# Delta-rule attention and a gelu feed-forward on one core: the first two chunks rebuilt

## The chip, the core and the metric

The kernel runs on one core of a Trainium2 chip. The metric is the device time of one execution in microseconds; the median of three runs is 825.52 us (823.81 to 825.66). The engines of the core work side by side: TensorE (PE in the profile, with PEld for its weight loads), VectorE (DVE), ScalarE (ACT), GpSimd (POOL) and SyncE (SP), which here only starts transfers.

## The reference

The first half is a delta rule for 4 batches and 8 heads, 768 positions and 48 channels a head. Every head has a state of 48 x 48; keys are normalized. The second half takes all heads of a position as a row of 384 and sends it through two weight matrices with a gelu between them.

```python
for t in range(S):
    kt, vt, bt = (k_n[:, :, t], v[:, :, t], beta[:, :, t, None])
    y[:, :, t] = np.einsum('bhd,bhde->bhe', q[:, :, t], state)
    v_old = np.einsum('bhde,bhd->bhe', state, kt)
    state = state + bt[:, :, :, None] * np.einsum('bhd,bhe->bhde', kt, vt - v_old)
...
x = attn_out.transpose(0, 2, 1, 3).reshape(B * S, H * D)      # 3072 x 384
h = x @ w_in                                                  # 384 x 2048
g = h * (1.0 / (1.0 + np.exp(-1.702 * h)))
return g @ w_out                                              # 2048 x 384
```

The two weight matrices arrive as 64-bit floats and have to be turned into 32-bit floats on the chip.

## The kernel before

**Units.** Positions are cut into 6 chunks of 128. A *unit* is one chunk of one batch, with all 8 heads; unit n is chunk n // 4 of batch n % 4, so there are 24. The units of one batch depend on each other through the state `ST`, those of one chunk do not. Two neighbouring units (`HB` = 2) are a *pair*, and the feed-forward takes a pair at a time.

**What a unit needs.** Keys (`KN`) are normalized (`normalize`, or `normalize_first` for the first seven), turned on TensorE and copied to `kT` (`transposed`). `prepare` (L350 on) multiplies `kT` with itself to the 128 x 128 scores `G` of each head, writes all of `G` to DRAM (`Nd`, 512 KB a unit) and reads back from it only the four 32 x 32 blocks on the diagonal of every head, into `NT`. There a row of 128 lanes holds a block: 4 batches x 8 heads x 4 blocks. `invert` (L389 on) solves these small triangular systems on DVE by substitution, in 25 parts that a caller can draw one after another: one product with beta, 15 rows, 4 and 4 products of quarters, and the last, which multiplies with beta again (`YS`) and takes the result through DRAM (`Yd`) into `XB`. For chunk 0 it runs once for all 128 lanes, for every later chunk twice, with the 64 lanes of a pair.

A `Step` then does the unit itself. `scores` turns the queries and makes `psQ` (the masked scores `M`, and for chunk 1 on the part of V that the state explains). The four blocks of 32 rows follow one another: `solve` multiplies V with `XB` on TensorE (`psU`), ScalarE copies the result to `US`, `below` makes what the block adds to later rows (`psR`), and DVE subtracts that from V (`rest`). `together` puts a `solve` of one unit beside a `below` of another. Last come `queries`, `outputs` and `state` (`psY`, `psS`). `outputs` puts the unit's row block into `xT`; a quarter of its rows goes there by transfers of 16 rows (`xT<-last`).

**Feed-forward.** `hidden` (x @ w_in and gelu, 16 portions a pair) and `written` (times w_out and out, 16 portions a pair) wait in `queue`, and `take` draws portions from it, so TensorE has them between the steps of the units.

**Order.** The kernel is written out as slots. Up to n = 5 `slot` has six groups (`GR`), each with some attention, some steps of `invert`, some conversions (`weights`, after the table `WB`) and some feed-forward; from n = 6 (`W`) `woven` has three stretches, spends 20.8 us of feed-forward a slot, and lets unit n + 1 begin, unit n go on and unit n - 1 end in the same slot. `follow` asks for later inputs, and puts a finished pair into the queue. In slots 0 and 1 and from 6 on the instructions keep the written order on their engines (`pinned`, seen as L105 in the profile); in between the compiler's planner orders them.

**Weights.** `from_double` makes a 32-bit float of the two words of a 64-bit one with four or five DVE instructions and one on ScalarE. A part is 512 columns of one third of w_in, or one of 16 row blocks of w_out. The raw words lie where w_out will be; `free` and `taken` say when a place may be filled again, and GpSimd's queue fetches.

**Before the first slot** (`warm(NW)` on) the keys of four units are normalized in two groups, their scores made and sent through DRAM, three parts of w_in converted, three units scored, and chunk 0's substitution run; matmuls without a result (`ps_warm`) keep TensorE running meanwhile.

Of the kernel before, what the change touches and what calls it, by code (L numbers as in the profile page):

```python
# [18 lines left out]
def kernel(  # L19
# [33 lines left out]
    GR = 6  # L53
    NTH = HB * C
    FQ = 4
    GB = 4

    W0, W1, WB = 3, 1, (1, 3, 5, 7, 8)
    NA = W0

    NW, NA0, NY, NB0 = 80, 3, 48, 6
    XR = DP - D
    W = 6
    NS = C * C + C
    assert S % C == 0 and H == 8 and D <= DP and DM == H * D == KC * 128
    assert B == 4 and B * H * NB == 128 and FC == 4 * FQ
# [40 lines left out]
    in_order, now = [False], [0]  # L107

    class Engine:
# [5 lines left out]
        def __getattr__(self, name):  # L115
            op = getattr(self.engine, name)
            return pinned(op) if in_order[0] else op

    vec, act, pe = Engine(nc.vector), Engine(nc.scalar), Engine(nc.tensor)

    for i in range(B):
        nc.vector.memset(KN[i][:, :, D:DP], 0.0)
        load(i, ((KN, k),))

    bI = cpool.tile([128, NC, BS], F32, name="bI")
    betas = beta.rearrange("b h (c k j) -> (b h) c k j", k=NB, j=BS)
    for blk in range(NB):
        nc.scalar.dma_start(out=bI[blk::NB], in_=betas[:, :, blk, :])


    ident = cpool.tile([128, 128], F32, name="ident")
    make_identity(nc, ident)
    half = cpool.tile([128, H], F32, name="half")
    nc.gpsimd.memset(half, 0.5)

    nc.gpsimd.memset(YB, 0.0)
    nc.gpsimd.affine_select(
        out=YB, in_=YB, compare_op=ALU.not_equal, fill=1.0, base=0,
        pattern=[[1, BS], [-1, BS]], channel_multiplier=0,
    )  # L140


# [5 lines left out]
    def warm(n, after=None):  # L148

        ps = ps_moe.tile([128, 256], F32, tag="moe", name="ps_warm")  # L150
        if after is not None:
            after(ps[:, 0:1], 0.0)
        for _ in range(n):
            pe.matmul(ps, lhsT=ones[:, 0:128], rhs=ones, start=True, stop=True)  # L154

    warm(NW)
    table = cpool.tile([128, 1], F32, name="table")
    nc.scalar.activation(table, ident[:, 0:1], ACT.Copy)

    w_in = cpool.tile([128, KC, DFF], F32, name="w_in")  # L160
# [3 lines left out]
    nc.gpsimd.memset(low, -896.0 * (1 << 23))  # L164

    def from_double(dst, raw, n, alone):

        lo, hi = raw[:, :, 0], raw[:, :, 1]
        ts, stt = vec.tensor_scalar, vec.scalar_tensor_tensor
        if alone:
            ts, stt = pinned(ts), pinned(stt)
        AND, OR = ALU.bitwise_and, ALU.bitwise_or
        E1 = 1 << 20
        p = dst.bitcast(I32)  # L180

        ts(p, hi, 0x7FF * E1, None, op0=AND)
        if alone:
            ts(p, p, -896.0 * E1, 0.0, op0=ALU.add, op1=ALU.max)
            ts(p, p, 255.0 * E1, 8.0, op0=ALU.min, op1=ALU.mult)
        else:
            act.activation(p, p, ACT.Relu, scale=8.0, bias=low)
        yield
        t = wk.tile([128, n], I32, tag="P", name="tmp")
        f = t.bitcast(F32)  # L190
        ts(t, hi, E1 - 1, E1, op0=AND, op1=OR)
        stt(out=f, in0=lo.bitcast(U32), scalar=2.0**-32, in1=t, op0=ALU.mult, op1=ALU.add)
        stt(out=p, in0=hi, scalar=-(1 << 31), in1=p, op0=AND, op1=OR)
        stt(out=dst, in0=f, scalar=2.0**-20, in1=dst, op0=ALU.mult, op1=ALU.mult)
        yield

    N_IN = 512
    parts_in = KC * DFF // N_IN
    n_parts = parts_in + FC

    x_rows = [
        (ct * DP + o, (ct * NP + i) * D, m, step)
        for ct in range(2)
        for o, i, m, step in ((0, 0, D, D), (D, KC, XR, XR))
    ]

    stages, taken, made, begun = {}, {}, [], {}  # L210

    def stage(part):

        if part < parts_in:
            at = part % (2 * KC) * 2 * N_IN
            return at, at + 2 * N_IN
        f = part - parts_in
        if f >= FC - 2:
            return None
        depth = 2 if f < 2 or f >= 8 else 4  # L220
        if f >= 12:
            depth = 1
        at = FC * DM // (2 if f < 2 else 1) - (f % depth + 1) * 2 * DM
        return at, at + 2 * DM

    def together_with(part):

        return list(range(part, part + (KC if part < 3 * KC else 1)))

    def free(part):  # L230
        places = [s for p in together_with(part) if (s := stage(p)) is not None]
        return all(s[1] <= a or b <= s[0] for s in places for a, b in taken.values())

    def fetch(part, dma):

        if part < parts_in:
            j, f0 = part % KC, part // KC * N_IN
            parts = together_with(part)
            shape, src = (len(parts), N_IN), moe_w_in[:, f0 : f0 + N_IN]
            dst = w_in[:, j : j + len(parts), f0 : f0 + N_IN]  # L240
        else:
            parts = [part]
            shape, src = (1, DM), moe_w_out
            dst = target(part)
        if src.dtype != F32:
            if (s := stage(part)) is None:
                raw = wk.tile([128, *shape, 2], I32, tag="xT", name="raw", bufs=3)
            else:
                words = slice(s[0], stage(parts[-1])[1])
                raw = w_out.rearrange("p f d -> p (f d)")[:, words].bitcast(I32)  # L250
                raw = raw.rearrange("p (j n o) -> p j n o", j=shape[0], o=2)
            for i, p in enumerate(parts):
                stages[p] = raw[:, i]
                if s is not None:
                    taken[p] = stage(p)
            dst = raw.bitcast(src.dtype).rearrange("p j n o -> p j (n o)")
        if part < parts_in:
            for i in range(len(parts)):
                for p, r, m, step in x_rows:
                    dma(out=dst[p : p + m, i], in_=src[r + (j + i) * step : r + (j + i) * step + m])  # L260
        else:
            r = (part - parts_in) * 128
            dma(out=dst if src.dtype == F32 else dst[:, 0], in_=src[r : r + 128, :])
        return parts

    def target(part):
        if part < parts_in:
            j, f0 = part % KC, part // KC * N_IN
            return w_in[:, j, f0 : f0 + N_IN]
        return w_out[:, part - parts_in, :]  # L270

    def begin(part):

        if part not in begun:
            if part >= parts_in:
                a, b = (part - parts_in) * DM, (part - parts_in + 1) * DM
                if any(taken[p][0] < b and a < taken[p][1] for p in stages if p in taken):
                    return
            dst = target(part)
            begun[part] = from_double(dst, stages[part], dst.shape[-1], part < NA)  # L280
            next(begun[part])

    def convert(part):
        if part in stages:
            begin(part)
            if staged:
                begin(min(staged))
            stages.pop(part)
            next(begun.pop(part))

            made.append(part)
            while made and (len(made) > 1 or part < NA or part >= n_parts - 8):
                taken.pop(made.pop(0), None)

# [20 lines left out]
    def normalize_first(b0, nb=HB):  # L315

        tt, ts = pinned(vec.tensor_tensor), pinned(vec.tensor_scalar)
        red, recip = pinned(vec.tensor_reduce), pinned(vec.reciprocal)
        stt = pinned(vec.scalar_tensor_tensor)
        mult, add = ALU.mult, ALU.add  # L320
        z = wk.tile([128, 4, nb, H], F32, tag="ksq", name="z", bufs=1)
        x, y, t, s = (z[:, i] for i in range(4))
        for b in range(nb):
            K = KN[(b0 + b) % len(KN)][:, :, 0:D]
            sq = wk.tile([128, H, D], F32, tag="G", name="sq", bufs=6)
            tt(sq, K, K, op=mult)
            red(s[:, b], sq, axis=AX.X, op=add)
# [8 lines left out]
        recip(s, s)  # L336
        for b in range(nb):
            K = KN[(b0 + b) % len(KN)][:, :, 0:D]
            tt(K, K, s[:, b].broadcast_to([128, H, D]), op=mult)

    def transposed(src, dst, early=False):

        pool_, tag = (ps_seq, "seq") if early else (ps_big, "big")
        psT = pool_.tile([128, NP, 128], F32, tag=tag, name="psT")
# [5 lines left out]
    def prepare(n):  # L350

        c, b = units[n]
        kn = KN[n % len(KN)]
        kT = wk.tile([128, NP, 128], F32, tag="kT", name="kT", bufs=6)
        transposed(kn, kT, c == 0)
        yield 0.6
        G = wk.tile([128, H, 128], F32, tag="G", name="G", bufs=6)
        pool_, tag = (ps_moe, "moe") if c == 0 and b % 2 else (ps_big, "big")
# [8 lines left out]
        if n < 2 * B + HB:  # L367
            act.activation(G[:, 1::2], ps[1], ACT.Copy)
        else:
            vec.tensor_copy(G[:, 1::2], ps[1])  # L370

# [357 lines left out]

    def slot(n, share):  # L730

# [197 lines left out]
```

## Time and profile before

| | |
|---|---|
| median of the timed runs | 825.52 us |
| the profiled execution, whole | 821.86 us |
| its span in the profile | 819.8 us |
| first scores on DVE / first `psU` on TensorE | 31.0 / 67.4 us |
| first `ph` of the feed-forward | 103.3 us |
| last `po` | 795.6 to 816.4 us |
| DVE, first 240 us, busy | 57.3 + 25.9 + 119.5 us |
| `w_out<-in_moe_w_out_dram`, 384 KB, issue to landing | 3.7 us median |
| `pow` on GpSimd | 2.2 us mean |

A matmul of 32-bit floats is two records in the profile: 96 records `ph` are the 48 matmuls of one pair. Rows of the timeline give start, duration, engine, line, operation, result and inputs with their shape, how many, and in square brackets how long the engine had been idle and what ended that. L105 is the line of the helper that pins an instruction, so names of tiles tell more than lines.

### The profile page before, as it was taken

What the parts mean: (1) busy time and instruction counts of PE and PEld (TensorE: products, weight loads), DVE (VectorE), ACT (ScalarE), POOL (GpSimd) and SP (SyncE); (2) the same over time, 40 slices, a digit from 0 to 9 for tenths busy, and PEclk for the clock granted to TensorE, in tenths of its full rate; (3) what the DMA queues carried; (4) which work ended last, traced back from release to release, by engine and by line L of the source; (5) the groups of instructions that cost most, each with busy time, mean ns of one, the idle gap of its engine ahead of it and who ended that gap; (6) DMA issues with size and microseconds to landing.
All of it is one profiled execution on the core that took longest, in us unless ns stands there. A gap on an engine that the chain in (4) does not pass through costs nothing.

```text
span 819.8 us, 18780 instructions
## 1 busy us (share of the span) xinstructions
PE 768.8 (94%) x8100; PEld 577.4 (70%) x8100; DVE 483.0 (59%) x1037; ACT 230.7 (28%) x499; POOL 131.7 (16%) x138
## 2 busy tenths in 40 slices
PE   8429799889799999999999999999999999999998
PEld 7327688557676876867867867867768768677684
DVE  7797989787965675666667667666656730100000
ACT  2212543242232332322422322322322223212120
POOL 2013120322021222122123122212201000000000
PEclk9659889978979999999999999999999999999999
DMA  7986732721315123214204213213222020000000
GB/s 146 199 183 122 201 87 82 178 68 48 68 30 125 34 49 96 60 23 100 62 21 102 53 32 90 54 43 80 53 59 45 12 51 1 11 16 1 24 1 19
DMA packets 147698, 55.96 MB, mean 68 GB/s; under 512 B 114720, under 2 KB 143616, under 8 KB 147616
## 3 DMA queue, kind: packets, MB, share of 16 engines
q1 hardware_dynamic: 139872, 41.96, 24.0%
q0 software_dynamic: 2752, 10.62, 4.7%
q10 hardware_dynamic: 4992, 2.20, 1.0%
q8 instruction: 63, 1.03, 0.6%
q14 instruction: 19, 0.16, 0.1%
HBM read 33.13 MB, written 20.45 MB: 65 GB/s over the span
## 4 chain that ended last, share of the span: by engine, by line
PE 79%; DVE 6%; issue 6%; DMA 4%; SPq 2%; POOL 1%; ACT 1%; DVEq 0%; POOLq 0%; ACTq 0%
PE po L105 28%; PE ph L105 25%; PE psY L105 5%; PE psU L105 4%; PE psQ L105 3%; PE ps_warm L154 3%; PE ph L633 2%; PE psG L105 2%; PE psR L105 2%; DMA w_out<-in_moe_w_out_dram 2%; PE psT L105 1%; SPq L105 1%; DMA w_out<-in_moe_w_in_dram 1%; DVE tmp L105 1%; PE psG L362 1%
## 5 line engine op out<-in xcount | busy, mean ns | idle before, releaser
L105 PE MATMUL po<-w_out,gT 128*128 128x384 f32 x704 | 239.3, 490 | 0.0
L105 PE MATMUL ph<-xT,w_in 128*128 128x256 f32 x966 | 222.0, 384 | 0.3
L105 PEld LDWEIGHTS ph<-xT,w_in 128*128 128x128 f32 x966 | 180.3, 191 | 30.9 <-issue 2.3
L105 PEld LDWEIGHTS po<-w_out,gT 128*128 128x128 f32 x704 | 130.1, 190 | 82.6 <-issue 1.9
L105 DVE TENSOR_TENSOR V<-V,psR 64x384 f32<-64x384 f32 (+1 forms) x80 | 44.4, 556 | 194.8 <-PE psR L105 194.0
L105 DVE TENSOR_TENSOR P<-NT,YB 64x18 f32<-64x18 f32 (+25 forms) x171 | 82.3, 481 | 4.5
L105 ACT ACTIVATE gT<-ph 128x512 f32<-128x512 f32 x81 | 48.2, 595 | 115.9 <-PE ph L105 115.8
L105 DVE TENSOR_REDUCE YB<-P 64x6 f32<-64x18 f32 (+25 forms) x171 | 72.7, 425 | 5.5
L105 ACT COPY US<-psU 32x384 f32<-32x384 f32 x80 | 37.6, 470 | 131.9 <-PE psR L105 118.4
L528 POOL TENSOR_SCALAR_AFFINE_SELECT M<-M 128x1024 f32<-128x1024 f32 x24 | 29.8, 1240 | 226.6 <-DVE M L105 159.8
L105 PEld LDWEIGHTS psU<-V,XB 32*32 32x32 f32 x1280 | 45.9, 105 | 27.9 <-issue 20.5
L105 PE MATMUL psU<-V,XB 32*32 32x48 f32 x1280 | 54.3, 203 | 2.1 <-DVE V L105 2.1
L105 PE MATMUL psR<-US,G 32*32 32x48 f32 x1920 | 52.8, 203 | 0.0
L633 PE MATMUL ph<-xT,w_in 128*128 128x128 f32 (+1 forms) x282 | 47.0, 321 | 1.6 <-DMA xT<-last 1.6
L105 PEld LDWEIGHTS psR<-US,G 32*32 32x32 f32 x1920 | 44.6, 105 | 0.5 <-issue 0.5
L633 PEld LDWEIGHTS ph<-xT,w_in 128*128 128x128 f32 x282 | 40.3, 198 | 5.7 <-issue 2.4
L154 PE MATMUL ps_warm<-ident 128*128 128x256 bf16 x152 | 22.8, 318 | 16.7 <-DVE ps_warm L105 14.4
L90 POOL DMA_DIRECT2D KN<-in_k_dram x14 | 13.4, 955 | 153.1 <-PE psY L105 102.0
L308 POOL TENSOR_TENSOR rn<-ssq,half 128x8 f32<-128x8 f32 x17 | 36.9, 2169 | 2.9 <-DVE ssq L306 2.9
L105 ACT COPY o<-po 128x384 f32<-128x384 f32 x22 | 10.5, 479 | 77.7 <-PE po L105 55.8
L154 PEld LDWEIGHTS <-ident 128*128 128x128 bf16 x152 | 17.1, 114 | 21.0 <-issue 14.6
L105 DVE TENSOR_TENSOR P<-NT 64x256 f32<-64x256 f32 (+7 forms) x36 | 30.3, 841 | 0.3
(144 smaller groups left out, 871.0 us busy)
## 6 DMA issues: line engine op xcount, KB each, us to landing
Nd<-G SPq DMA_DIRECT2D x20, 512.0 KB, 3.5
w_out<-in_moe_w_out_dram POOLq DMA_DIRECT2D x14, 384.0 KB, 3.7
QP<-in_q_dram SPq DMA_DIRECT2D x24, 192.0 KB, 3.9
V<-in_v_dram SPq DMA_DIRECT2D x24, 192.0 KB, 3.0
out_dram<-o SPq DMA_DIRECT2D x24, 192.0 KB, 1.9
w_out<-in_moe_w_in_dram SPq DMA_DIRECT2D x18, 192.0 KB, 5.2
NT<-Nd SPq DMA_DIRECT2D x24, 128.0 KB, 2.6
Yd<-YS SPq DMA_DIRECT2D x24, 128.0 KB, 2.5
```

Of the source, the lines that this page charges most:

```text
L90: dma(out=dst[n % len(dst)][:, :, 0:D], in_=src[b, :, c * C : (c + 1) * C, :].rearrange("h p d -> p h d"),)
L105: return lambda *a, **kw: tc.keep_in_program_order(op(*a, **kw))
L154: pe.matmul(ps, lhsT=ones[:, 0:128], rhs=ones, start=True, stop=True)
L308: nc.gpsimd.tensor_tensor(rn, ssq, half, op=ALU.pow)
L362: pe.matmul(ps[h % 2][:, h // 2], lhsT=kT[r, h // 2, :], rhs=kT[r, h // 2, :], start=True, stop=True,)
L528: nc.gpsimd.affine_select(out=self.M, in_=self.M, compare_op=ALU.is_gt, fill=0.0, base=0, pattern=[[0, H], [1, 128]], channel_multiplier=-1,)
L633: pe.matmul(ph[:, u], lhsT=w_in[:, j, f * 128 : (f + 1) * 128], rhs=xT[:, j, t], start=(j == 0), stop=(j == KC - 1),)
```

## The change

Everything up to the middle of chunk 1 is written anew, as one sequence in which all DVE, ScalarE and TensorE instructions are pinned; `slot`, `weights` and the places' bookkeeping are gone, and `woven` now begins at n = 7.

- Keys of units 0 to 3 are normalized in one group; squares on ScalarE. A new `diagonal` makes the 32 x 32 blocks directly, and only these go through DRAM (128 KB a unit, on ScalarE's queue). The full scores `G` are made afterwards, during the substitution, and stay on the chip for chunk 0.
- Raw w_in comes in quarters, of which two are fetched at the start, w_out in row blocks. `conversions` is one sequence of 100 small steps in a fixed order, and `fill(n)` draws n of them. `fetches` says which piece's end asks for which raw block. Most raw blocks lie in w_out's place, some in free `G` and `xT` buffers.
- Units 0 to 3 run side by side as two alternating chains of two (`hops`), with one conversion step in each of eight rounds. Unit 3's `US` lies in w_in's last quarter, its `QS` and `M` in `gT` buffers, of which there are now 8.
- Then x @ w_in of all four units runs with four conversion steps a portion, and between them the keys of units 4 to 7 are prepared.
- `invert(1)` takes chunk 1's four units in one run of 128 lanes, beside w_out of the four units; then a chain of units 4 and 5 alone, whose feed-forward runs beside a chain of 6 and 7, two portions a round.
- The keys of units 4 to 11 are normalized by `normalize_mixed`: square on ScalarE, power and product on GpSimd, pinned.

```diff
-    GR = 6
...
-    GB = 4
+    GB = 8
...
+    def diagonal(b, D_):
+        kT = kTs[b]
+        ps = [ps_seq.tile([128, NP, BS], F32, tag="seq", name="psD") for _ in range(2)]
+        for h in range(H):
+            r = slice(h % 2 * 64, h % 2 * 64 + D)
+            for blk in range(NB):
+                u = slice(blk * BS, (blk + 1) * BS)
+                pe.matmul(
+                    ps[h % 2][u, h // 2, :], lhsT=kT[r, h // 2, u], rhs=kT[r, h // 2, u],
+                    start=True, stop=True,
+                )
+        for e in range(2):
+            act.activation(D_[:, e::2, :], ps[e], ACT.Copy)
...
+    def conversions():
+        whole = list(pieces())
...
+        after = begin(0)
+        yield
+        for i in range(len(whole)):
+            ops = after
+            next(ops)
+            yield
+            next(ops)
+            yield
+            if i + 1 < len(whole):
+                after = begin(i + 1)
+                yield
+            next(ops)
+            yield
+            next(ops)
+            done.add(whole[i][3])
+            fetches.pop(whole[i][3], lambda: None)()
+            yield
+
+    fetches = {
+        ("in", 1): lambda: fetch_in(2),
+        ("in", 3): lambda: fetch_in(3),
+        ("in", 5): lambda: (fetch_out(0), fetch_out(1)),
+        ("in", 7): lambda: (fetch_out(2), fetch_out(3), fetch_out(4), fetch_out(5)),
+        ("out", 3): lambda: (fetch_out(6), fetch_out(7), fetch_out(9), fetch_out(12)),
+        ("out", 5): lambda: fetch_out(8),
+        ("out", 7): lambda: (fetch_out(10), fetch_out(11), fetch_out(13)),
+        ("out", 9): lambda: fetch_out(14),
+        ("out", 12): lambda: fetch_out(15),
+    }
...
+    def normalize_mixed(n):
+        K = KN[n % len(KN)][:, :, 0:D]
...
+        act.activation(ksq, K, ACT.Square)
+        yield 0.0
...
+        vec.tensor_reduce(ssq, ksq, axis=AX.X, op=ALU.add)
...
+        pool.tensor_tensor(rn, ssq, half, op=ALU.pow)
+        yield 0.0
+        vec.tensor_scalar(rn, rn, 1e-6, None, op0=ALU.add)
+        vec.reciprocal(rn, rn)
+        pool.tensor_tensor(K, K, rn.broadcast_to([128, H, D]), op=ALU.mult)
+        yield 0.0
...
+    warm(80)
+    normalize_first()
+    Ds = spare("blocks").rearrange("p (b h j) -> p b h j", b=B, j=BS)
+    Nds = []
+    for b in range(B):
+        turn(b)
+        diagonal(b, Ds[:, b])
+        Nd = dram.tile([H * C * BS], F32, tag="Nd", name="Nd", bufs=4)
+        beside(out=Nd.rearrange("(h p k) -> p h k", p=C, k=BS), in_=Ds[:, b])
+        Nds.append(Nd)
...
+    fill(9)
+    for b in range(B):
+        gram(b)
+        warm(3)
+    pair = [new_step(n) for n in range(B)]
...
+    run(invert(0))
+    fill(5)
+
+    def hops(a, b):
+        yield [(a, 0)], []
+        for blk in range(NB - 1):
+            yield [(b, blk)], [(a, blk)]
+            yield [(a, blk + 1)], [(b, blk)]
+        yield [(b, NB - 1)], []
...
+    paths = hops(*pair[:2]), hops(*pair[2:])
+    warm(10)
+    for i in range(2 * NB):
+        for path in paths:
+            together(*next(path))
+        fill(1)
...
+    def other_work():
+        for n in range(B, 2 * B):
+            for _ in normalize_mixed(n):
+                yield
+            for _ in prepare(n):
+                yield
+
+    other = other_work()
+    ffn = [hidden(xTs[0], first, slice(0, NTH), 1.3), hidden(xTs[1], second, slice(0, NTH), 1.3)]
+    for f in range(FC):
+        for part in ffn:
+            next(part)
+        fill(4)
+        next(other, None)
...
+    run(other)
+    run(converting)
+    for i, gT in enumerate((first, second)):
+        queue.append(written(*units[i * HB], gT))
...
+    inverting = invert(1)
+    pair = [new_step(n) for n in (B, B + 1)]
+    for i in range(25):
+        ahead_of(inverting, 1)
+        step()
...
+    for n in (8, 9):
+        for _ in normalize_mixed(n):
+            step()
+        for _ in prepare(n):
+            step()
...
+    chain(*pair, lambda i: None)
+    enqueue(2)
...
+    def more(i):
+        ahead_of(inverting, 2)
+        step()
+
+    chain(*pair, more)
+    enqueue(3)
...
-    for n in range(-1, len(units) + 1):
-        in_order[0], now[0] = n < HB or n >= W, n
-        step = slot if n < W else woven
-        step(n, 15.6 if n <= B else 18.8 if n <= B + HB else 20.8)
+    next(new_step(8).scored)
+    for n in range(7, len(units) + 1):
+        woven(n, 20.8)
     run(take(1e9))
```

## Prediction

> **What bounds the kernel now.** I read the page's busy rows and slices first, then a table by stages, the timeline of the first 70 us, the timeline around 380 us and that of the end.
>
> ```profile
> span 819.8 us, 18780 instructions
> PE 768.8 (94%) x8100; PEld 577.4 (70%) x8100; DVE 483.0 (59%) x1037; ACT 230.7 (28%) x499; POOL 131.7 (16%) x138
> ...
> PE   8429799889799999999999999999999999999998
> ...
> DVE  7797989787965675666667667666656730100000
> ...
> PEclk9659889978979999999999999999999999999999
> ```
>
> ```profile
> 0.00:67.44 67.44, 38.48 (x298) 30.95 (x299) 57.30 (x140) 15.67 (x32) 13.14 (x32) 0.72 0.96 177
> 67.44:99.00 31.56, 25.95 (x540) 20.98 (x541) 25.85 (x53) 15.31 (x30) 5.47 (x10) 0.95 0.61 152
> 99.00:240.00 141.00, 128.21 (x1353) 98.69 (x1350) 119.48 (x266) 47.51 (x105) 30.38 (x32) 0.87 0.36 85
> 240.00:382.50 142.50, 142.39 (x1627) 104.84 (x1626) 88.90 (x183) 41.99 (x93) 28.92 (x23) 1.00 0.28 66
> ```
>
> The first fence is the page; the second is the table by stages: the stretch, its length, then busy time of PE, PEld, DVE, ACT and POOL, the granted clock and the DMA. From 240 us TensorE has no gap, so the rebuilt part can gain only before that. 0 to 67 us is preparation: DVE is busy 57 of 67, and TensorE's 38 hold 23 of warm-up matmuls. From 99 to 240 TensorE is busy 128 of 141, at clock 0.87.
>
> ```profile
> 31.00 1.22 DVE L105 TENSOR_TENSOR NT<-NT,bI 128x1024 f32<-128x1024 f32 x1 [3.11 <-DMA NT<-Nd]
> ...
> 57.88 1.23 DVE L456 TENSOR_TENSOR YS<-YB,bI 128x1024 f32<-128x1024 f32 x1
> ...
> 67.44 0.86 PE L105 MATMUL psU<-V,XB 32*32 32x48 f32 x16
> ```
>
> ```profile
> 381.78 2.85 PE L105 MATMUL po<-w_out,gT 128*128 128x384 f32 x8
> 384.46 4.05 PE L105 MATMUL ph<-xT,w_in 128*128 128x256 f32 x18
> ```
>
> ```profile
> 774.91 20.88 PE L105 MATMUL ph<-xT,w_in 128*128 128x256 f32 x96
> 795.63 20.80 PE L105 MATMUL po<-w_out,gT 128*128 128x384 f32 x64
> ```
>
> Scores reach DVE at 31.0, the substitution takes 26.9 (25.8 without 1.1 of conversion between), and its result is used at 67.4. A pair of units costs 20.8 + 20.8 = 41.6 us of feed-forward. At 382.5 four pairs are all but done (2.8 us of `po` remain), unit 9 is out, and `woven(11)` begins. The new program reaches exactly that state at the end of its `woven(10)`, with an empty queue; what follows is the same code. So the forecast is one date: when does it get there, against 382.5?
>
> [...] 0.50 in 40 to 60 us, where TensorE was busy 5 of 20. [...] The trace shows 144 and 202 GB/s in its first two 20 us.
>
> **Start to first solve.** Removed: SyncE's wait chain on four 512 KB `Nd` writes (5.0 us for the last). Added: 4 x 32 score products of 32x32. The trace has none; bounds are `psR`, 48 records in 0.81 (17 ns each), and `psU`, 16 in 0.79 (49 ns): 64 records cost 1.1 to 3.1 us, I take 1.3. A unit is then a loop through two engines: transpose 0.44, `kT` copy 0.6, products 1.3, two copies 0.55, issue 0.4, in all 3.1 us by ScalarE's order. Four from 13.9 (end of the warm-up) end at 26.5; a 128 KB write and read (2.5 each by `Yd`, 3 under the load of 6 MB fetched at once) give 33 (29 to 36). One normalization of four units (12 us) is covered by the warm-up. Substitution 25.8, `YS` 1.2, four writes and reads through DRAM 6.5: first solve at 66, as before. That part is worth nothing. The warm-up matmuls that go (48 behind a memset, 6 a group) ran where TensorE had nothing else: nothing either, unless the clock falls.
>
> **Four units side by side.** Eight rounds, each two subtractions or four of 0.55 plus one conversion step on DVE: 3.1 x 2 + 2.0 x 4 + 1.5 x 2 = 17.2 us; outputs 4 x (1.1 + 0.6) and copies, 8. Done at 91; before, only units 0 and 1 are out by about 120. This is the gain: some 19 us of TensorE work ahead. But `xT<-last` issues (12 x 0.6, behind 12 issues of `fetch_in(3)`) let the feed-forward begin at 99: 8 idle.
>
> **x @ w_in of four units.** TensorE needs 41.3 + 3 x 1.54 (turn, gram) = 46. DVE has steps 27 to 90 of the conversions: at 512 wide a piece costs 2 x 0.42 + 3 x 0.69, so 4.3 at 768 and 2.4 at 384 (per element as before): 44 us, plus 3.3 for norms, whose squares now run on ScalarE (0.5 each, beside gelus). `late_U`, unit 3's result kept in `w_in`, holds step 29 until unit 3 is out at 91, which is when DVE gets there: nothing. Alone that would fit. But a raw piece is fetched only when an earlier one is converted, and is asked for 1.6 to 3 us later, while such a fetch takes 3.7 to 5 (page: 3.7 median): six waits of 1.2 to 3.5, 15 us. The order binds both: `turn(5)` stands after the norms of unit 5, these behind DVE's step 54, which lies at 127 by that sum, when TensorE could be there at 122; it stands 10 us. Unit 7's square comes behind the last gelu, then 0.5 + 0.6 + 1.9 (`pow`) + 0.4 + 0.9 + 0.6 in a row with TensorE idle. The stage ends at 164 (150 if nothing waits).
>
> **Second substitution and chain 4, 5.** One at 128 lanes replaces two at 64: DVE saves 26 us, all of it hidden, because beside it TensorE has 41.6 of w_out, 4.8 of scores and 3.1 of grams: 49.5, to 214. Then the queue is empty and one chain runs bare: 2 x 2.05 + 4 x 1.5 + 2.4 = 12.5, outputs 4.1 + 1.1, `xT` 3.7 + 1.8: feed-forward again at 238. Of 24 us, 12 are work.
>
> **Units 6, 7 and to the common state.** 40 steps of 1.29 = 51.6, attention 18.7, latencies and clock 5: 313. `woven(7)` has 16 steps: 25. Only 8 steps remain for `woven(8)`: 17. `woven(9)` and `(10)` have none, and DVE's substitution sets them: DVE is busy 37 to 38 us per two slots in the trace's steady part, with waits 40, where TensorE has 17. Sum 82: the state is reached at 395, 12.5 us after before. The first `xT` then comes without cover: 2 more.
>
> **Sum.** 819.8 + 14.5 = 834.3 span; the profiled execution took 821.86, 2.1 more, so 836.4. The three timed runs have a median of 825.52; with the same difference 840, and I say 839.
>
> **Rivals.** (1) *The w_in pass keeps TensorE's pace* (faster). If the raw pieces land before DVE asks, the 15 us of waits go, TensorE doesn't stand at `turn(5)`, and its clock stays up (3 us): the stage ends at 148 to 150. With scores at 29 as well (the cheap end of the products), that is 16 + 4 off: 840 - 20 = 820. For: 384 KB landed in 3.7 median, and TensorE alone needs only 46. Against: each request is tied to a conversion just done. It decides from 17 us off on, so when the waits sum to below 2 us and the scores come by 30. (2) *The bare stretches cost more* (slower): the clock halves in the chain of 4 and 5, in `woven(9)` and `(10)`[...]; ten more on TensorE's 60 us of work there, and the four loaded transfers add 8: 858. For: 0.50 in 40 to 60. Against: the small matmuls keep TensorE partly busy. (3) *Cancelled*: early gain equals late loss, 825: the same kind of account with 14 us less waiting in any stage. (4) *It doesn't do what it says*: the pinned order makes TensorE wait for conversions in the chain of 0 to 3, so that side by side gains nothing: four bare chains of 12.5 for 17, 840 + 33 = 873. Against: a round's DVE sum is only 3 us.
>
> **Chances.** Forecast 0.55; (1) 0.20; (2) 0.16; (3) 0.05; (4) 0.04. A difference of 0.3% is about what a measurement can tell from none: faster 0.20, within 0.05, slower 0.75. The forecast's own range, from the bounds of the score transfers (4 either way), the waits (14 down, 6 up) and the late stage (6), is 826 to 850. Reaching to the others it is 814 to 864.
>
> **What would show it.** Right: DVE's `NT` product near 33; the first `psU` near 66; first `ph` record near 95 to 99; DVE waiting on DMA `w_out` and `raw` between 105 and 150; TensorE idle before `psT` of units 5 and 7; a gap of some 12 us between the last early `po` and the next `ph`; after it, two slots near 350 to 395 at half TensorE load with DVE full. Wrong: the state (fourth pair's last `po`, then `ph`) before 375, or no wait on `w_out`, or TensorE full in `woven(9)`. If DVE runs its substitution ahead of TensorE there, the 22 us I charge for those two slots are gone and the sign turns.

## The result: 995.63 us, ratio 1.207

The changed kernel takes 995.63 us (median of four runs, 994.12 to 999.01), the kernel before it 825.59 us in the same session. The ratio is 1.2071, 95% interval 1.2034 to 1.2107. The forecast was 839, its range 814 to 864. The direction was right; the size was missed by 157 us.

The page of the changed kernel, its busy rows and slices:

```profile
span 992.9 us, 18720 instructions
PE 810.9 (82%) x8126; PEld 618.1 (62%) x8126; DVE 445.1 (45%) x904; ACT 237.6 (24%) x511; POOL 117.0 (12%) x121
...
PE   6474888798789999469869959959959968979888
...
DVE  4465667474224656882383284184085073020000
...
PEclk8575689899699999669969969959978978989999
```

TensorE has the same matmuls to do (8126 records, before 8100), and DVE is busy even 38 us less than before. Yet TensorE now sits idle for 992.9 - 810.9 = 182 us (before: 51), and is busy 42 us longer at a lower clock (0.859 in the mean, before 0.952). The new thing in the slices is the teeth from the middle on: TensorE and its clock dip every third slice, and DVE swings between 8 and 0. That part of the program is `woven`, nearly the same lines as before.

So the loss has two parts. Both kernels pass through one state, the first `ph` of the fifth pair. Before, it stood at 384.5 and the rest took 435.3; now it stands at 444.9 and the rest takes 548.0. That is 60.4 us lost up to there, and 112.7 behind it. The chain of waits shows what happens behind it (start, length, engine, tile, line, count):

```profile
444.90 20.92 PE ph L101 x96
465.82 20.64 PE po L101 x64
488.54 0.91 POOL KN L290
490.96 2.07 PE psY L101 x48
...
512.78 3.60 PE psY L101 x48
...
521.24 21.08 PE ph L101 x96
542.32 20.64 PE po L101 x64
```

All 96 records of x @ w_in of a pair follow one another, then all 64 of w_out: 41.6 us in which TensorE does nothing of the attention. DVE works on its substitution for the first 11 of them and then stands for 31.8 us, until TensorE makes the next `psR`. Then the next two slots' attention runs with no feed-forward beside it. From one pair to the next it takes 76.3 us, and from the fifth pair's first `ph` to the last pair's it is 500.96 us, 71.6 for each of seven intervals. Before, these seven take 390.45, 55.8 each. Seven times 15.8 is 111 us, so this alone is nearly all of the 112.7.

The stages of the same kernel (stretch, length, busy time of PE, PEld, DVE, ACT, POOL, clock, DMA):

```profile
400.00:420.00 20.00, 10.83 (x232) 9.24 (x232) 16.12 (x46) 4.16 (x10) 5.45 (x4) 0.57 0.28 60
420.00:440.00 20.00, 10.36 (x209) 8.93 (x206) 16.95 (x30) 5.17 (x13) 5.52 (x5) 0.60 0.23 50
...
460.00:480.00 20.00, 20.00 (x72) 13.47 (x72) 0.00 (x0) 2.27 (x4) 0.00 (x0) 1.00 0.03 10
480.00:500.00 20.00, 13.99 (x257) 9.97 (x257) 11.90 (x23) 5.87 (x13) 2.67 (x3) 0.97 0.26 67
500.00:520.00 20.00, 12.47 (x250) 10.58 (x248) 16.12 (x30) 5.29 (x13) 5.38 (x4) 0.60 0.15 30
```

From 400 to 440 `woven(9)` and `woven(10)` have no feed-forward to draw, as forecast: DVE is busy for 16 to 17 of 20 us, TensorE half idle, at clock 0.57 to 0.60. From 460 to 480 it is the other way round: DVE does nothing at all. From 500 to 520 comes the first picture again, though by then there is feed-forward that could have been kept for it.

The early part, in the timeline (start, length, engine, line, operation, result and inputs, and in brackets how long the engine was idle before and what ended that):

```profile
4.08 7.89 ACTq L101 DMA_DIRECT2D bI<-in_beta_dram  x3
12.02 0.94 ACT L101 ACTIVATE squares<-KN 128x384 f32<-128x384 f32 x2 [9.71 <-DMA bI<-in_beta_dram]
31.53 4.59 ACTq L101 DMA_DIRECT2D NT<-Nd  x4
36.22 1.76 ACT L101 ACTIVATE w_in<-w_in,low 128x768 int32<-128x768 int32 x2 [5.21 <-DMA NT<-Nd]
37.19 0.96 DVE L101 SCALAR_TENSOR_TENSOR w_in<-w_out,w_in 128x768 int32<-128x768 int32 x1 [13.66 <-ACT w_in L101]
41.87 1.23 DVE L101 TENSOR_TENSOR NT<-NT,bI 128x1024 f32<-128x1024 f32 x1 [0.27 <-DMA bI<-in_beta_dram]
69.20 0.86 DVE L101 TENSOR_TENSOR P<-NT 128x256 f32<-128x256 f32 x1 [8.23 <-ACT NT L101]
76.49 1.22 DVE L101 TENSOR_TENSOR YS<-YB,bI 128x1024 f32<-128x1024 f32 x1
85.61 1.45 PE L101 MATMUL psU<-V,XB 32*32 32x48 f32 x16 [16.24 <-DMA XB<-Yd]
88.87 1.37 PE L101 MATMUL psU<-V,XB 32*32 32x48 f32 x15 [1.82 <-DMA XB<-Yd]
```

(ACTq is ScalarE issuing transfers.) The scores reach the substitution at 41.9 instead of 33, its last product on DVE (`YS`) starts at 76.5, and the first `psU` starts at 85.6 instead of 66. ScalarE stands in front of DVE three times: it issues transfers before the squares (7.9 us for three of beta) and before the conversion's step that DVE waits for (13.7 us), and inside the substitution a copy of ScalarE stands behind other copies (8.2 us). Whether the order of its work is the cause is asked below, one piece at a time.

### The profile page after: what moved, and what is told of

Same layout as the page of the kernel before. It is cut to its first block, busy times and chain, and to the rows that moved or that the text cites. A ratio compares the mean times of both kernels' runs of the same rounds, so it can differ in the third digit from the quotient of the medians.

```text
span 992.9 us, 18720 instructions
## 1 busy us (share of the span) xinstructions
PE 810.9 (82%) x8126; PEld 618.1 (62%) x8126; DVE 445.1 (45%) x904; ACT 237.6 (24%) x511; POOL 117.0 (12%) x121
## 3 DMA queue, kind: packets, MB, share of 16 engines
q1 hardware_dynamic: 137296, 47.35, 21.5%
q8 instruction: 64, 1.05, 0.5%
HBM read 33.13 MB, written 18.87 MB: 52 GB/s over the span
## 4 chain that ended last, share of the span: by engine, by line
PE 69%; DVE 13%; DMA 6%; SPq 4%; ACT 4%; issue 2%; POOL 2%; ACTq 0%; POOLq 0%; DVEq 0%
PE ph L101 24%; PE po L101 24%; PE psY L101 6%; DVE P L101 4%; PE psU L101 4%; SPq L101 3%; PE psQ L101 3%; PE psG L101 3%; PE psR L101 3%; DVE V L101 2%; PE psT L101 2%; DVE YB L101 2%; DMA w_out<-in_moe_w_in_dram 2%; DVE NT L101 1%; DMA xT<-last 1%
## 5 line engine op out<-in xcount | busy, mean ns | idle before, releaser
L101 PE MATMUL ph<-xT,w_in 128*128 128x256 f32 x1152 | 270.4, 395 | 25.9 <-DMA xT<-last 20.4
L101 PE MATMUL psU<-V,XB 32*32 32x48 f32 x1536 | 93.7, 236 | 39.1 <-DMA XB<-Yd 18.4
L101 PEld LDWEIGHTS psU<-V,XB 32*32 32x32 f32 x1536 | 81.0, 129 | 58.5 <-issue 23.9
L101 DVE TENSOR_TENSOR P<-NT,YB 64x8 f32<-64x8 f32 (+31 forms) x190 | 88.1, 464 | 5.8 <-DVE YB L101 0.3
L101 DVE TENSOR_REDUCE YB<-P 64x4 f32<-64x8 f32 (+31 forms) x190 | 80.9, 426 | 6.5
L101 PE MATMUL psR<-US,G 32*32 32x48 f32 x2208 | 78.1, 237 | 4.3 <-ACT US L101 1.9
L101 PE MATMUL psQ<-QS,kT 48*128 48x176 f32 (+1 forms) x384 | 40.5, 359 | 21.0 <-ACT QS L101 20.1
L101 ACT COPY o<-po 128x384 f32<-128x384 f32 x24 | 11.5, 479 | 186.5 <-PE po L101 184.1
L101 PEld LDWEIGHTS psQ<-QS,kT 48*128 48x128 f32 x384 | 33.4, 220 | 26.2 <-ACT QS L101 25.5
L101 PE MATMUL psG<-kT 48*128 48x128 f32 x384 | 36.2, 342 | 1.5 <-ACT kT L101 1.4
L101 PEld LDWEIGHTS psG<-kT 48*128 48x128 f32 x384 | 31.1, 242 | 7.4 <-ACT kT L101 2.6
```

What stands on the lines that cost most here:

```text
L101: return lambda *a, **kw: tc.keep_in_program_order(op(*a, **kw))
```

## The experiments

Two theories stood for the late part. **Debt**: `spend` books what a slot may draw and subtracts what was drawn. Where the queue is empty nothing is subtracted, and the booking stays.

```python
debt = [0.0]
def spend(cost):
    debt[0] += cost
    for done in take(debt[0]):
        debt[0] -= done
```

`woven(8)`, (9) and (10) book 20.8 each and find, by the forecast's count, 8 portions: 62.4 - 10.4, some 52 us of debt. The first `spend` after the fifth pair has entered the queue may draw all of the pair's 41.6 us at once. The queue is then empty again. Two slots book 41.6 us, just one pair, so the debt is never worked off, and so on to the last pair. **DVE's rate** was the rival: the attention of two slots takes DVE about 40 us with its waits, and something else in the new program could keep it from running ahead of TensorE.

### Clearing the debt

```diff
         for done in take(debt[0]):
             debt[0] -= done
+        if not queue:
+            debt[0] = 0.0
```

> The changed kernel; only spend is changed, so that what it could not draw from an empty queue is forgotten. Debt theory (slots 9 and 10 run with an empty queue, their 20.8 us each stay owed, and from slot 11 on a whole pair of feed-forward is drawn at once while the next slots have none): the stretch from the fifth pair's first ph to the end goes back from 548 us to 435 as in the kernel before, so about 113 us less, 880 to 885. Rival (the late slots are slow in themselves: DVE's substitution and a low clock set 77 us a pair, whatever stands between): no change, 985 to 995.

Measured: 883.72 us (882.95 to 884.97), ratio 1.0741 (1.0686 to 1.0796), 112 us less than the changed kernel. The fifth pair's first `ph` stands at 445.4, where it was, and from there to the end it takes 435.8 us; the kernel before takes 435.3. The table by stages of this kernel, for the stretch shown above:

```profile
460.00:480.00 20.00, 19.90 (x233) 15.46 (x232) 13.36 (x23) 6.86 (x15) 4.53 (x4) 1.00 0.23 54
480.00:500.00 20.00, 20.00 (x245) 13.13 (x244) 13.42 (x21) 4.57 (x11) 3.44 (x4) 1.00 0.17 45
500.00:520.00 20.00, 20.00 (x198) 16.33 (x200) 12.61 (x38) 6.38 (x13) 4.52 (x3) 1.00 0.36 80
```

DVE works evenly beside a full TensorE. TensorE's idle time falls from 182 to 881.2 - 774.3 = 107 us and its busy time by 37, with the clock at 1.00 in these stretches: 75 + 37 is the 112.

### The same debt in the kernel before

```diff
-    debt = [0.0]
+    debt = [60.0]
```

> The kernel before; only the debt that woven starts with is 60 us instead of 0. Debt theory: the first late slot empties the queue, and from then on every pair's 41 us of feed-forward stand in one block and the attention of two slots stands bare behind it; some 18 us a pair for eight to nine pairs, 960 to 980. Rival (the early rebuilt part or its buffers cause the slow late slots): the kernel before has none of these, so 820 to 830.

Measured: 975.41 us, ratio 1.185 (1.1771 to 1.1929). One number costs some 150 us, in a program to which nothing else was done. Its chain of waits shows the same blocks for every pair from the third on; here are the fifth and the sixth:

```profile
431.77 20.96 PE ph L105 x96
452.73 20.64 PE po L105 x64
475.45 0.91 POOL KN L312
...
511.74 20.92 PE ph L105 x96
532.66 20.64 PE po L105 x64
```

So the debt alone makes the teeth; nothing of the rebuilt chunks is needed for it.

### The front, one piece at a time

What is left, about 60 us, was sought in the early part, on top of the cleared debt. First beta before everything else:

```diff
+    for blk in range(NB):
+        beside(out=bI[blk::NB], in_=betas[:, :, blk, :])
     ident = cpool.tile([128, 128], F32, name="ident")
...
-    for blk in range(NB):
-        beside(out=bI[blk::NB, 0], in_=betas[:, 0, blk, :])
-    for blk in range(NB):
-        sync(out=bI[blk::NB, 1:], in_=betas[:, 1:, blk, :])
```

> As the run with the debt forgotten, and all of beta is requested on ScalarE's queue before anything else of ScalarE, as in the kernel before, in place of after the raw weights. Theory ([...] the squares come at 12 us, and the first NT product waits for beta's last transfer at 41.9): squares near 5 us, NT product at 34 to 37, the end 5 to 8 us earlier than with the debt forgotten alone. Rival (the NT product waits on the conversion steps ahead of it, which wait on ScalarE's queue): NT product still after 40, end within 3 us.

Measured, a single run: 883.19 us, no difference that one run could show. The timeline of ScalarE:

```profile
0.81 2.62 ACTq L101 DMA_DIRECT2D bI<-in_beta_dram  x4
...
4.87 0.51 ACT L101 ACTIVATE squares<-KN 128x384 f32<-128x384 f32 x1
...
14.73 0.52 ACT L101 ACTIVATE squares<-KN 128x384 f32<-128x384 f32 x1 [5.30 <-DMA KN<-in_k_dram]
```

The first square starts at 4.9 instead of 12.0, but the last of the four waits for its keys until 14.7, and the product with `NT` stays at 41.3. The beta issues were a wait in front of a later one.

Then the half-block copy in the first substitution on DVE instead of ScalarE:

```diff
-        act.activation(X1, halves(Y)[1].rearrange("p l i -> p i l"), ACT.Copy)
+        (vec.tensor_copy(X1, halves(Y)[1].rearrange("p l i -> p i l")) if c == 0 else act.activation(X1, halves(Y)[1].rearrange("p l i -> p i l"), ACT.Copy))
```

> As the run with the debt forgotten, and in chunk 0's substitution the copy of the second half block is made by DVE instead of ScalarE. Theory (the copy stands behind twelve to sixteen score copies on ScalarE, and DVE waits 8.2 us for it): the gap goes, YS begins 7 to 8 us earlier, the end comes 5 to 8 us earlier. Rival (what follows is late anyway, the transfers of XB beside the raw weights): YS earlier, first psU within 3 us of where it was, end within 3 us.

Measured, a single run: 881.98 us. The gap of 8.2 us is gone, but the product with `NT` came 3.2 us later in this run than in the run with the debt forgotten (44.4 and 41.2), `YS` starts 3.0 us earlier (72.4 and 75.4), and the first `psU` 2.4 (82.5 and 84.9). The expected 5 to 8 us at the end are not there.

Then both, and besides them a new order of the requests at the start. Only the first quarter of raw w_in is asked for behind the first keys, and the score reads are on SyncE's queue. `QP`, `V`, the second quarter and the later keys are asked for behind the score reads (the two edits above are in it too and not shown again):

```diff
-    fetch_in(0, other_queue)
...
+    fetch_in(0)
...
-        beside(
+        sync(
             out=NT[b * NB * H : (b + 1) * NB * H].rearrange("d i k -> d (i k)"),
...
+    for b in range(B):
+        load(b, ((QP, q),), sync)
+    for b in range(B):
+        load_values(b, sync)
+    fetch_in(1, other_queue)
+    for n in range(B, len(KN)):
+        load(n, ((KN, k),), sync)
```

> As the run with the debt forgotten, with beta requested first, the half-block copy on DVE, and the requests at the start in the order of the kernel before: after the keys only the first quarter of raw w_in on SyncE's queue, the four reads of the diagonal blocks on SyncE's queue as well, then queries, values, the second quarter and three keys. Theory (6 MB asked for at once hold back the fourth batch of keys to 14.7 us and the four reads hold ScalarE and with it the conversions and the NT product to 41): keys by 8, NT product at 30 to 33, first psU at 70 to 73 in place of 85, the end 10 to 13 us earlier, 869 to 874. Rival (the small score products and their transfers are the length of that chain, wherever they queue): NT product not before 38, end not before 880.

Measured: 881.56 us (881.52 to 881.6), ratio 1.0693: a miss, 2 us below the run with the debt forgotten. The rival's dates came true (`NT` product after 38, end after 880), but not for its reason. The keys were normalized early, but the substitution was not, and the timeline says why:

```profile
45.59 0.69 DVE L101 TENSOR_SCALAR w_in<-w_out 128x768 int32<-128x768 int32 x1 [14.64 <-DMA w_out<-in_moe_w_in_dram]
46.20 1.21 DVE L101 TENSOR_TENSOR NT<-NT,bI 128x1024 f32<-128x1024 f32 x1
```

DVE waits 14.6 us for the second raw quarter of w_in, which this edit requests later. `fill(9)` stands in front of the substitution, and its ninth step is the first of the third piece, which reads that quarter. The instructions are pinned, so the scores wait behind this step while DVE waits for weights that nobody needs yet.

### The late feed-forward spread

Instead of clearing the debt, the queue can be kept from running empty, without a change to `spend`: fewer portions beside the chain of 6 and 7 and beside the keys of 10 and 11, and a smaller share per slot up to n = 10.

```diff
     def more(i):
         ahead_of(inverting, 2)
-        step()
...
             ahead_of(inverting, 2)
             step()
-            step()
...
-        woven(n, 20.8)
+        woven(n, 12.35 if n < 11 else 20.8)
```

> The changed kernel with spend as it is and only the portions of feed-forward spread otherwise: one portion in place of two beside each round of the chain of units 6 and 7 and beside the norms of units 10 and 11, and 12.35 us a slot in slots 7 to 10 in place of 20.8, so that 26 + 38 = 64 portions last exactly to the end of slot 10 and the queue is never empty. Debt theory: no debt is left over, the late part runs as in the kernel before without any change to spend, and the bare slots 9 and 10 are covered too: 10 to 18 us below the run with the debt forgotten, 865 to 875. Rival (the debt was only half of it, and the new order needs spend's catching up): above 885.

Measured: 870.24 us, ratio 1.0555 (1.0499 to 1.0612): 125 us less than the changed kernel, and 13 less than with the cleared debt. From 400 to 460 TensorE is now busy for 59.2 us at clock 1.00; with the cleared debt it was 39.9 at 0.72. With the reordered front of the last section as well:

> Both of the last two. Additive: 852 to 862. If both only move the same wait: no better than the better of the two.

Measured: 865.66 us (864.78 to 866.55), ratio 1.05: neither of the two forecasts. The reordered front gave 2 us alone and gives 4.6 here, so the two add up, but the front's gain that the sum counted on had not come: DVE again waits 14.75 us for the second raw quarter.

### More matmuls for the clock

From 80 to 120 us, where the four units run, TensorE's clock is 0.50 to 0.64. Matmuls without a result were put in front of the rounds, and six into each step of both chains, so twelve a round where the forecast below speaks of six. All of it is on top of the last kernel:

```diff
-    warm(10)
+    warm(60)
     for i in range(2 * NB):
         for path in paths:
             together(*next(path))
+            warm(6)
         fill(1)
```

> As the run with both, and matmuls without result to hold TensorE's clock: 60 in place of 10 before the chains of units 0 to 3, and 6 in each round. Clock theory (rounds of 3 us where DVE's sum is 2 to 3, and psR and psU at 0.5 to 0.58 of the clock): clock near 1.0 in the chains, eight rounds in 17 to 20 us in place of 26, the end 5 to 9 us earlier than without. Rival (DVE and the hand-overs set the rounds): end within 2 us, or later by the 8 x 0.65 us of added matmuls.

Measured: 882.93 us, 17 more than without them. The table by stages, first of the kernel without the added matmuls, then with them:

```profile
80.00:100.00 20.00, 13.40 (x449) 12.22 (x452) 9.36 (x15) 4.96 (x10) 0.00 (x0) 0.50 0.54 85
100.00:120.00 20.00, 16.56 (x328) 15.97 (x322) 12.29 (x20) 8.28 (x22) 0.00 (x0) 0.64 0.40 85
```

```profile
80.00:100.00 20.00, 17.45 (x345) 12.80 (x348) 5.98 (x10) 3.74 (x7) 0.00 (x0) 0.56 0.50 73
100.00:120.00 20.00, 20.00 (x340) 14.56 (x336) 6.87 (x11) 4.22 (x8) 0.00 (x0) 0.50 0.09 26
```

TensorE shows 17 and 20 us of work in 20, and the clock stays at 0.56 and 0.50. What stands in front of the rounds, in the timeline of TensorE with the added matmuls:

```profile
70.76 7.05 PE L101 MATMUL ps_warm<-ident 128*128 128x256 bf16 x63
82.55 1.46 PE L101 MATMUL psU<-V,XB 32*32 32x48 f32 x16 [4.74 <-DMA XB<-Yd]
```

The block in front ran at clock 1.00, from 70.8 to 77.8. Then TensorE stood for 4.7 us until `XB` came. The clock is 1.00 from 76 to 80, 0.82 from 80 to 84 and 0.50 from 84 to 120, so the rounds ran at 0.50. So the forecast that these matmuls bring the clock back in the rounds fell; six of them took 1.46 us at that clock, about half of what TensorE shows, and each step of the chains became longer by them. That a block reaching up to the first `psU` would have held the clock is not excluded: that was not tried.

### Eight steps instead of nine

```diff
-    fill(9)
+    fill(8)
...
     run(invert(0))
-    fill(5)
+    fill(6)
```

> The new kernel with keys and betas first and late feed-forward spread (865.7), and one more edit: eight conversion steps instead of nine stand in front of the first substitution, the ninth behind it. Theory (the pinned ninth step, which needs the second raw quarter, held DVE until 45.6 while the scores lay ready): NT product at 30 to 32, YS at 57 to 59, first psU at 67 to 70, first ph at 104 to 109, timed 848 to 855. Rival 1 (the early lead is taken back by the x @ w_in pass, whose raw quarters then arrive late): first psU at 67 to 70, but timed 858 to 866. Rival 2 (the score chain itself is late): NT product at 38 or later.

Measured: 852.63 us (851.3 to 853.61), ratio 1.035 (1.0334 to 1.0366): 13 us for one step moved. The timeline of this kernel:

```profile
30.45 1.23 DVE L101 TENSOR_TENSOR NT<-NT,bI 128x1024 f32<-128x1024 f32 x1 [0.31 <-DMA NT<-Nd]
57.56 1.22 DVE L101 TENSOR_TENSOR YS<-YB,bI 128x1024 f32<-128x1024 f32 x1
...
104.98 2.93 PE L101 MATMUL ph<-xT,w_in 128*128 128x256 f32 x6 [3.20 <-DMA xT<-last]
```

DVE now waits 0.3 us, and for the scores themselves. The first `psU` stands at 66.9, where the forecast had it.

### Keeping w_out for the bare chain

The chain of units 4 and 5 runs without cover, since w_out of the first four units is drawn beside the substitution before it. Here it is drawn at half the rate:

```diff
         ahead_of(inverting, 1)
-        step()
+        if i % 2 == 0:
+            step()
...
         for _ in normalize_mixed(n):
-            step()
+            pass
```

> The run with eight steps in front, and w_out of units 0 to 3 is drawn at half the rate beside the second substitution, so that some 17 of its 32 portions are left for the chain of units 4 and 5. Theory (that chain runs bare because its cover was used up before): TensorE busy over 95 per cent of the 30 us of that chain instead of some 70, first ph of the third pair 10 to 18 us earlier, timed 832 to 843, no faster than the kernel before. Rival (DVE and ScalarE set the length there, TensorE's portions only move): less than 4 us of difference to the run with eight steps.

Measured: 856.34 us (851.77 to 859.72): no gain over 852.63, and the four runs of this kernel spread by 8 us. The chain is covered, TensorE is full from 238 to 265 at clock 1.00. But what was in front of it lost its cover, as the timeline of TensorE shows:

```profile
201.84 2.72 PE L101 MATMUL psQ<-QS,kT 48*128 48x176 f32 x16 [7.31 <-ACT QS L101]
...
220.73 1.12 PE L101 MATMUL psT<-ident,KN 128*128 128x128 f32 x4 [8.22 <-POOL KN L101]
231.86 1.12 PE L101 MATMUL psT<-ident,KN 128*128 128x128 f32 x4 [2.59 <-POOL KN L101]
```

The idle time moved from the chain to the substitution and to the keys of 8 and 9. The expected 10 to 18 us for the third pair became a delay: its first `ph` is at 274.6 instead of 260.9. Some 3.5 us of that delay stood already at the first `ph` (108.5 instead of 105.0), in front of the edit. The rival's words fit: the portions only move. As laid out here, they don't cover both places.

### No raw w_out to wait for

In the x @ w_in pass DVE waits for raw blocks of w_out. The three long waits, and two of TensorE's in the same pass, in the timeline of the kernel with eight steps in front:

```profile
121.93 0.56 DVE L101 TENSOR_SCALAR w_out<-w_out 128x768 int32<-128x768 int32 x1 [7.62 <-DMA w_out<-in_moe_w_out_dram]
127.62 0.56 DVE L101 TENSOR_SCALAR w_out<-w_out 128x768 int32<-128x768 int32 x1 [1.81 <-DMA w_out<-in_moe_w_out_dram]
138.35 0.56 DVE L101 TENSOR_SCALAR w_out<-w_out 128x768 int32<-128x768 int32 x1 [3.05 <-DMA w_out<-in_moe_w_out_dram]
130.66 5.45 PE L101 MATMUL ph<-xT,w_in 128*128 128x256 f32 x24 [1.03 <-ACT gT L101]
140.41 5.49 PE L101 MATMUL ph<-xT,w_in 128*128 128x256 f32 x12 [4.30 <-ACT gT L101]
```

TensorE waits for gelus (`gT`), 1.03 and 4.30 us. In the written order a conversion's step, which needs a result of DVE, stands in front of the next portion's gelus on ScalarE; that DVE's waits reach TensorE this way was my estimate. The kernel tried here leaves out the fetches of w_out:

```diff
-            words = wk.tile([128, 2 * DM], I32, tag=outside[f], name="raw", bufs=6 if outside[f] == "G" else 3)
+            words = raws[:, 0 : 2 * DM] if f > 13 else raws[:, 14 * DM : 16 * DM]
...
-        sync(out=as_rows(places[f])[:, 0], in_=moe_w_out[f * 128 : (f + 1) * 128, :])
```

> The run with eight steps in front, but w_out is never fetched: its conversions work on the words that lie on the chip, with the same shapes and in the same order, so the second half of the feed-forward multiplies with meaningless weights. DVE then has no transfer to wait for in the x @ w_in pass, where it waited 7.6, 1.8 and 3.1 us. Theory (those waits reach TensorE, as the forecast took them to, 15 us of them on a stage of 66): the stage from the first ph to the scores of unit 7 ends 8 to 13 us earlier, timed 840 to 846. Rival (TensorE's pace there is set by its own 46 us, the gelus and unit 7's chain, and DVE's waits lie beside it): less than 4 us, timed 849 to 854.

Measured: 845.35 us (844.41 to 845.87), 7.3 less than with the fetches; its ratio to the kernel before is 1.0249 (1.0218 to 1.028). From the first `ph` to the scores (`psG`) of unit 7 it takes 166.1 - 106.5 = 59.6 us instead of 174.7 - 105.0 = 69.8. TensorE's two waits for `gT` are gone. So these waits do reach TensorE: 12.5 us on DVE are worth 10 in the stage, and 7 at the end. The run takes away the transfers' load as well as the waits (HBM reads fall from 33.13 to 26.84 MB), so the 7 us are what the fetches cost in all.

## Why the prediction was wrong, step by step

**The step that failed** is that the new program reaches "exactly that state" with an empty queue, and that "what follows is the same code". The code is the same, its state was not. I had forecast that `woven(9)` and `(10)` "have none", that is, no steps to draw, and took over the remaining 437 us of the profile before all the same, without asking what `spend` does with a share that it can't draw. It keeps it. The forecast has the fifth pair's first `ph` at 395 + 2 = 397, and 834.3 - 397 = 437.3 us behind it; that took 548.0: 110.7 of the 158.6 us by which the span was missed. Clearing the debt gives 112 back, and the rest then takes 435.8; adding a debt to the kernel before costs 150. Both show it. None of the rivals had this mechanism, and so the range was as wrong as the value.

**The other 47.9 us** are missed sizes on the way to that first `ph`, 444.9 instead of 397 (all in us):

| step | forecast | measured | later by |
|---|---|---|---|
| scores reach DVE (`NT` product) | 33 | 41.9 | 8.9 |
| from there to the first `psU` | 33 | 43.7 | 10.7 |
| to the first `ph` | 33 | 37.4 | 4.4 |
| to the end of the x @ w_in pass | 65 | 70 | 5 |
| w_out and the chain of 4 and 5, to `ph` | 74 | 84.5 | 10.5 |
| to the start of `woven(7)` | 75 | 74.4 | -0.6 |
| `woven(7)` to `(10)` | 82 | 91.5 | 9.5 |
| to the first `ph` of the fifth pair | 2 | 1.5 | -0.5 |

- *Start to first solve.* "That part is worth nothing" was wrong by 20 us. The products were not the cause: 64 records `psD` took 0.89 us where I took 1.3, and the loop of a unit 2.65 where I took 3.1. What I left out is the queues. I counted what ScalarE's queue saves SyncE, and not what its own DMA issues hold up: the squares, and the `Relu` step of a conversion on which DVE stands for 13.7 us in front of the substitution. A pinned conversion that others wait for I named only in rival (4), for the chain of units 0 to 3, and put no price on it here. The run with eight steps reaches the first `psU` at 66.9, so the forecast's date can be had, and the order of the requests, of one copy and of one conversion step is what it cost. That it is just this date is luck in part: the scores come 2.5 us earlier than I took (30.5 for 33), the substitution and its transfers take 3.4 longer (36.4 for 33).
- *Four units side by side.* Done at about 122, 36 us after the first `psU`; I took 25. The rounds took about 26 us instead of 17.2. I timed each round by DVE's subtractions alone, but a round is a loop through TensorE too: DVE waits for `psR` before most of them. 16 records `psU` take 1.45 us at 85.6, where the clock is 0.50, and took 0.86 in the kernel before at 67.4, where it was 1.00. 1.8 us more are the wait for the second `XB`. How the rest divides between the clock and the hand-overs no run shows. The gain that I expected from there (a first `ph` at 99 instead of 103) never came: it stands at 123, and even with the front mended at 105.
- *The x @ w_in pass.* Close: 70 us for 65. DVE's waits on raw w_out came to some 11.5 us in four, where I took 15 in six, and the run without fetches shows that they cost TensorE about 10. Rival (1) needed just this stage to be free of waits. It fails on the measured waits, and with the debt and the front mended and no fetches at all the time is still 845.
- *Second substitution and the chain.* DVE's 26 us saved are hidden, as forecast. But the stage in front of the chain took 59 us instead of 50: TensorE idles 6.7 us of it between 213 and 253, in part for the keys of 8 and 9 on GpSimd, and the chain behind it ran at clock 0.51 (253 to 267). What I left out is that the portions of w_out have the latencies of all these steps to cover; the run that kept half of them back bared those, and gained nothing.
- *`woven(9)` and (10)*: the picture was right, DVE nearly full and TensorE half idle, and rival (2) was right about the clock there, 0.57 to 0.60. The four slots took 9.5 us longer than forecast. How much of that is the clock no run separates.

Of the rivals, (4) came nearest by its number, 873, though still 123 us off, and its mechanism, a pinned conversion that others wait behind, cost 13 us, but in front of the first substitution and not in the chain of 0 to 3. Rival (2), 858, named the loaded transfers and the clock of the bare stretches; with the debt cleared the kernel is still 26 us above it, at 884. The best version of the change, 852.6 us, is still 3.5% above the kernel before. Its TensorE idles 850.9 - 775.8 = 75 us, 24 more than before, and is busy 7 more. Of that difference 7 us go with the fetches of w_out, as the last run shows. The rest was not taken apart by a run, and its cause stays open. TensorE is not full in the chain of 4 and 5 (21.5 us of work in 32 us from 230 to 262, at clock 0.68) and in the rounds of the first four units (clock 0.50 to 0.55). No version tried here beats the kernel before.

## What to carry to other kernels

When a stage is moved into code that stays, ask what state that code carries over: a budget that books work it could not draw will draw it all later, in one block. As long as its queue is never empty, the program doesn't show this. Take over a measured duration only after checking that each variable which sets the order enters with the value it had. And where the order is pinned, look among the instructions in front of the critical one for one that waits for something late: a single step of nine waited 14.75 us for its transfer here, and moving it was worth 13 us.

## What the runs showed of the hardware that was not expected

- Issues held their engine for up to 12.1 us. Four transfers of beta that ScalarE asks for before anything else took 2.6 us in the run with beta first. In the changed kernel one was issued first, and the other three, beside the requests for raw w_in, took 7.9, with a DMA share of 1.02 and 1.17 in the first two stretches of 20 us. Six issues of SyncE for raw w_in took 12.1 there, and 6.5 in the run with beta first. Why they took longer there no view shows.
- The clock came back in one stretch of work and not in another. In the kernel before, a block of matmuls without a result begins at 58.0 at clock 0.50; the clock is 0.50 until 62, 0.89 from 62 to 64 and 1.00 from 64, and with up to twelve such matmuls between the steps of its chain it stays at 1.00 from 68 to 80. In the run with the added matmuls the clock is at 0.50 from 84, after TensorE's pause of 4.7 us, and there TensorE shows work without a gap from 84 to 120, half of it matmuls of 32 x 32, at 0.50 all along. Whether the small matmuls are what makes the difference was not tried.
